# k weights in two blocks of whole rows, and another order of the first four tiles

## The chip, the cores and the metric

The kernel runs on one core of a Trainium2 chip. The metric is device time in microseconds, the median of several executions. The core's engines are TensorE (PE, matmuls and transposes, with its weight loads shown as PEld), VectorE (DVE), ScalarE (ACT), GpSimd (POOL) and SyncE (SP). Each runs its own instructions strictly in the order in which they were written; semaphores make one engine wait for another. Transfers are issued from the queue of an engine, here SP's or ACT's, and are carried out by 16 DMA engines.

## The reference

The input x has 2048 rows of 640 values in bf16. The output is x plus two parts, A and B:

```python
def _A_ref(x, wqkv, wo):            # x: layer norm of the input
    qkv = (x @ wqkv).reshape(B, S, 3, H, Dh)   # 32 heads of 20
    phi = lambda t: jnp.where(t > 0, t + 1, jnp.exp(t)) + 1e-6
    pq, pk = phi(q), phi(k)
    kv = jnp.einsum("bhsd,bhse->bhde", pk, v)
    z = jnp.einsum("bhsd->bhd", pk)
    num = jnp.einsum("bhqd,bhde->bhqe", pq, kv)
    den = jnp.einsum("bhqd,bhd->bhq", pq, z)[..., None] + 1e-6
    return (num / den) @ wo
def _B_ref(x, w_r, w_gate, w_up, w_down):
    r = x @ w_r                     # router; the 8 highest rows
    y = (silu(x_sel @ w_gate) * (x_sel @ w_up)) @ w_down * sigmoid(r_sel)
    return x with y added to the 8 rows chosen
return x + _A_ref(layernorm(x), ...) + _B_ref(x, ...)
```

## The kernel before

The 2048 rows are 16 tiles of 128 rows, t = 0 to 15. In a first phase each tile goes through these steps, each a small Python function:

- `ld` (line 103) loads x of the tile into XX.
- `ln_a`, `ln_b` (151, 154) take the statistics of columns 0 to 319 and 320 to 639 on DVE, `ln_g` (157) joins them, `ln_r` (160, 161) makes the reciprocal deviation with two ACT instructions, `ln_xn` (165) writes the normed tile on DVE.
- `tr_mm` (174) transposes a part of the normed tile on PE into a bank of PSUM (h = 0: two blocks of 128 columns, h = 1: three), and `tr_cp` (181 on ACT, 183 on DVE) copies it to xnT. Tiles 0 to 3 go this way. From tile 4 on `tr_dma` (186) transposes by a DMA on SP's queue.
- `ones` (267) sets one column of the normed tile to one on POOL.
- `K` (210) multiplies xnT of the tile by the k weights wk. It has two halves of 320 output columns (`hs`), in two banks, and each half five matmuls, one per block of 128 weight rows. `KA` is blocks 0 and 1, `KB` blocks 2 to 4. The right half has one more column: the router's weights, put into wk by an ACT copy (line 135) from a transposed w_r.
- `PHe` and `PHr` (226, 229) take exp and relu of a half of K from PSUM on ACT; `PHb` (245) joins both halves to pk on DVE. That is phi(k).
- `G` (254, 261) accumulates the product of the normed tile and pk in PSUM, over all tiles: nine matmuls per tile. `rcopy1` (241) copies tile 1's router column.

For tiles 0 to 3 the order of all these is a list of calls written out by hand, interleaving the tiles; since an engine works in order, the list fixes each engine's order. From tile 4 a loop follows: `K(t)`, `ones(t)`, `PHb(t-1)`, `ln_xn(t+2)` and `tr_dma(t+2)`, `PHe`/`PHr` of t, the statistics of t+3 and t+4, `G(t-1)`. Statistics, norm and transposes of tiles 4 and 5 stand in the list by hand.

After this phase come q (line 482), the key-value products, the experts of part B and the output (line 754). They are not touched. Bank numbers in the list (`6`, `4`, `0`, `2`) say which PSUM bank a step uses, so a bank must be read out before the next matmul starts in it: K of tile 1 uses banks 4 and 5, K of the others 6 and 7, transposes 0 to 3, and G uses banks 0 to 5.

The k weights lie in wk with 768 columns per block of rows. Before the change the left half is in columns 0 to 319, the right one from column 384, and they are loaded as two transfers, the left on ACT's queue, the right on SP's behind x of tiles 1 to 3. Each weight row is a piece of 640 bytes.

Of the kernel before, what the change touches and what calls it, by code (L numbers as in the profile page):

```python
# [7 lines left out]
P = 128  # L8
S = 2048
D = 640  # L10
# [4 lines left out]
KC = D // P  # L15
# [15 lines left out]
F32 = mybir.dt.float32  # L31
I32 = mybir.dt.int32
I16 = mybir.dt.int16
AF = mybir.ActivationFunctionType
# [4 lines left out]
def kernel(  # L39
# [12 lines left out]
    nc = tc.nc  # L52
    pe, dve, act, pool, sp = nc.tensor, nc.vector, nc.scalar, nc.gpsimd, nc.sync

    x_v = A_x[0].rearrange("(t p) d -> p t d", p=P)
    out_v = out[0].rearrange("(t p) d -> p t d", p=P)
    wqkv_v = A_wqkv.rearrange("(kc p) n -> p kc n", p=P)

    sb = ctx.enter_context(tc.tile_pool(name="sb", bufs=1))
    tmp = ctx.enter_context(tc.tile_pool(name="tmp", bufs=2))  # L60
# [6 lines left out]
    def st(shape, dt, name, tag=None):  # L67
        return sb.tile(shape, dt, name=name, tag=tag or name)

    XX = st([P, T, 2, D], BF16, "XX")  # L70
# [3 lines left out]
    wk = st([P, KC, WS], BF16, "wk", "wkM")  # L74
# [21 lines left out]
    MR = st([P, T], F32, "MR")  # L96

    HW = 320
    wkh = [wk[:, :, 0:HW], wk[:, :, HW + 64 :]]


    def ld(eng, dst, src):
        eng.dma_start(dst, src)
# [4 lines left out]
    dve.memset(MVf[:], 0.0)  # L108
    wr = st([KC, P], BF16, "wr")
    ld(act, wr[:], B_w_r.rearrange("(kc p) -> kc p", p=P))  # L110
    ld(act, wkh[0], wqkv_v[:, :, D : D + HW])
    ld(sp, XX[:, 1, 1, :], x_v[:, 1, :])
    ld(sp, XX[:, 2, 1, :], x_v[:, 2, :])
    ld(sp, XX[:, 3, 1, :], x_v[:, 3, :])
    ld(sp, wkh[1][:, :, 0:HW], wqkv_v[:, :, D + HW : 2 * D])
    for a, b in ((4, 8), (8, 12), (12, 16)):
        ld(sp, XX[:, a:b, 1, :], x_v[:, a:b, :])
    sp.dma_start_transpose(xnT[:, 0:4, S - P : S], zero[:])
# [1 line left out]
    def warm4(w):  # L120
# [6 lines left out]
        out=ident[:], in_=ident[:], compare_op=ALU.not_equal, fill=1.0,  # L127
# [18 lines left out]

    sts = {}

    def ln_a(t):
        sts[t] = tmp.tile([P, 2, nc.vector.BN_STATS_DIM], F32, tag="stats", name="stats", bufs=4)  # L150
        dve.bn_stats(out=sts[t][:, 0, :], in_=XX[:, t, 1, 0:320])  # L151

    def ln_b(t):
        dve.bn_stats(out=sts[t][:, 1, :], in_=XX[:, t, 1, 320:D])  # L154

    def ln_g(t):
        dve.bn_aggr(out=MV[:, t, :], in_=sts[t][:])

    def ln_r(t):
        act.activation(lnv[:, t : t + 1], MV[:, t, 1:2], AF.Ln, bias=eps5[:])  # L160
        act.activation(SR[:, t : t + 1], lnv[:, t : t + 1], AF.Exp, scale=-0.5)  # L161

    def ln_xn(t, parts=((0, D),)):
        for a, b in parts:
            dve.tensor_scalar(out=XX[:, t, 0, a:b], in0=XX[:, t, 1, a:b], scalar1=MVf[:, t, 0:1],  # L165
                              scalar2=SR[:, t : t + 1], op0=ALU.subtract, op1=ALU.mult)
# [3 lines left out]
    def tr_mm(t, h, b0):  # L170
        k0, k1 = TRP[h]
        pt = PS[:, b0 + h, :].bitcast(BF16)
        for kc in range(k0, k1):
            pe.transpose(pt[:, (kc - k0) * P : (kc - k0 + 1) * P], XX[:, t, 0, kc * P : (kc + 1) * P], ident[:])  # L174

    def tr_cp(t, h, b0, eng):
        k0, k1 = TRP[h]
        src = PS[:, b0 + h, :].bitcast(BF16)[:, 0 : (k1 - k0) * P].rearrange("p (k c) -> p k c", c=P)
        dst = xnT[:, k0:k1, t * P : (t + 1) * P]
        if eng is act:  # L180
            act.copy(dst, src)
        else:
            dve.tensor_copy(dst, src)

    def tr_dma(t):
        sp.dma_start_transpose(xnT[:, :, t * P : (t + 1) * P], XX[:, t, 0, :])
# [14 lines left out]
    def off(t, h):  # L201
        return T - 1 - t if t != 1 and h else 0

    def K(t, hs=(0, 1), b=6, ks=range(KC)):
        for h in hs:
            if t > 4:
                pad(1)
            w = HW + h
            for kc in ks:
                pe.matmul(  # L210
                    PS[:, b + h, off(t, h) : off(t, h) + w],
                    lhsT=xnT[:, kc, t * P : (t + 1) * P],
                    rhs=wkh[h][:, kc, 0:w],
                    start=(kc == 0),
                    stop=(kc == KC - 1),
                )

    phis = {}

    def phi_src(t, h, b):  # L220
        return PS[:, b + h, off(t, h) : off(t, h) + HW]

    def PHe(t, h, b=6):
        if t not in phis:
            phis[t] = tuple(tmp.tile([P, D], BF16, tag=k, name=k, bufs=3) for k in ("ek", "rk"))
        act.activation(phis[t][0][:, h * HW : (h + 1) * HW], phi_src(t, h, b), AF.Exp)  # L226

    def PHr(t, h, b=6):
        act.activation(phis[t][1][:, h * HW : (h + 1) * HW], phi_src(t, h, b), AF.Relu)  # L229

    def PHa(t, hs=(0, 1), b=6):
        for h in hs:
            PHe(t, h, b)
            PHr(t, h, b)
# [5 lines left out]
    def rcopy1(b):  # L240
        act.copy(rbf[:, T - 2 : T - 1], PS[:, b, HW : HW + 1])

    def PHb(t):
        ek, rk = phis[t]
        dve.scalar_tensor_tensor(out=pk[:, t, :], in0=ek[:], scalar=1.0, in1=rk[:], op0=ALU.min, op1=ALU.add)  # L245

    def pad(n):
        for _ in range(n):
            pe.ldweights(zero[:, 0:P])  # L249

    def G(t, ks=range(KC)):
        for a in ks:
            lhsT = XX[:, t, 0, a * P : (a + 1) * P]
            pe.matmul(  # L254
                PS[:, a, :], lhsT=lhsT, rhs=pk[:, t, 0:512],
                start=(t == 0), stop=(t == T - 1),
            )
            if t > 4:
                pad(2)
            if a < 4:  # L260
                pe.matmul(  # L261
                    PS[:, 5, a * P : (a + 1) * P], lhsT=lhsT, rhs=pk[:, t, 512:D],
                    start=(t == 0 and a == 0), stop=(t == T - 1), skip_group_check=True,
                )

    def ones(t):
        pool.memset(XX[:, t, 0, ZD : ZD + 1], 1.0)  # L267
# [23 lines left out]
    def bm2_copies(gs):  # L291
        for g in gs:
            pool.tensor_copy(bm2[32 * g : 32 * g + 32, :], bm2[0:E2, :])
# [43 lines left out]
    consts_e()  # L337
    bm2_copies((1, 2, 3))
    KA, KB = (range(0, 2), range(2, KC))
    ln_a(0)  # L340
    ln_b(0)
    ln_a(1)
    ln_g(0)
    ln_b(1)
    ln_r(0)
    ln_g(1)
# [5 lines left out]
    tr_cp(0, 0, 0, act)  # L352
    tr_mm(0, 1, 0)
    ones(0)
    ln_a(2)
    tr_mm(1, 0, 2)
    tr_cp(0, 1, 0, act)
    K(0, (0,), 6, KA)
    ln_b(2)
    tr_cp(1, 0, 2, act)  # L360
    tr_mm(1, 1, 2)
    ones(1)
    K(0, (0,), 6, KB)
    tr_cp(1, 1, 2, act)
    ln_g(2)
    ln_a(3)
    K(1, (0,), 4, KA)
    ln_r(2)
    ln_b(3)
    K(1, (0,), 4, KB)  # L370
    PHe(0, 0, 6)
    ln_xn(2)
    K(0, (1,), 6, KA)
    PHr(0, 0, 6)
    K(1, (1,), 4, KA)
    ln_g(3)
    ln_r(3)
    tr_mm(2, 0, 0)
    K(0, (1,), 6, KB)
    tr_cp(2, 0, 0, act)  # L380
    tr_mm(2, 1, 0)
    ones(2)
    ln_xn(3)
    K(1, (1,), 4, KB)
    PHe(0, 1, 6)
    tr_cp(2, 1, 0, dve)
    PHr(0, 1, 6)
    tr_mm(3, 0, 2)
    ln_a(4)
    K(2, (0,), 6, KA)  # L390
    rcopy1(5)
    PHe(1, 0, 4)
    tr_mm(3, 1, 2)
    ones(3)
    PHb(0)
    K(2, (1,), 6, KA)
    PHr(1, 0, 4)
    K(2, (0,), 6, KB)
    PHe(1, 1, 4)
    K(2, (1,), 6, KB)  # L400
    ln_b(4)
    PHr(1, 1, 4)
    PHe(2, 0, 6)
    G(0, (4,))
    tr_cp(3, 0, 2, dve)
    ln_g(4)
    G(0, (0,))
    PHr(2, 0, 6)
    tr_cp(3, 1, 2, dve)
    G(0, (1,))  # L410
    ln_r(4)
    PHb(1)
    G(0, (2,))
    K(3, (0,), 6, KA)
    PHe(2, 1, 6)
    G(0, (3,))
    ln_xn(4)
    PHr(2, 1, 6)
    K(3, (0,), 6, KB)
    ln_a(5)  # L420
    tr_dma(4)
    ones(4)
    K(3, (1,), 6, KA)
    ln_b(5)
    PHe(3, 0, 6)
    G(1)
    PHr(3, 0, 6)
    ln_g(5)
    PHb(2)
    ln_r(5)  # L430
    ln_xn(5)
    K(3, (1,), 6, KB)
    tr_dma(5)
    ones(5)
    G(2)
    PHe(3, 1, 6)
    PHr(3, 1, 6)
    ln_a(6)
    ln_b(6)
    ln_g(6)  # L440
# [515 lines left out]
```

## Time and profile before

| What | Value |
|---|---|
| Median of 3 runs | 106.52 us (106.29 to 106.86) |
| Profiled execution | 106.34 us |
| Its span, first to last instruction | 104.6 us |
| TensorE's granted clock | 1.000 |
| PE busy | 99.7 us, 95% of the span |
| DVE busy | 82.8 us, 79% |
| ACT busy | 68.8 us, 66% |
| Right half of the k weights, issue to landing | 5.4 us |

The profiled execution's time has some 1.7 us around its span. Rows of a timeline give start, duration and what ran, with the idle time before it and what ended that in brackets. The chain of the work that ended last gives at each step the instruction that held up the next one. The profile numbers lines by the kernel's file; a helper has one line for all its calls.

### The profile page before, as it was taken

To read this page: it belongs to the slowest core of one execution; us is meant where nothing else is said; L and a number is where in the kernel's file an instruction comes from. 1 tells how busy PE (TensorE), PEld (TensorE's weight loads), DVE (VectorE), ACT (ScalarE), POOL (GpSimd) and SP (SyncE) were. 2 spreads that over 40 slices of the span, in tenths; PEclk is the share of its full clock that TensorE was granted. 3 is DMA by queue.
4 is the path that set the end of the run, shared out by engine and by line. 5 is a ranking of instruction groups with operands and counts; after the bars stand their busy time and mean duration, and the time that the engine had idled before them with its cause. 6 is when DMAs were issued, how large, how long until landed. Compare 5 with 4: busy or idle time off the path is not lost.

```text
span 104.6 us, 2773 instructions
## 1 busy us (share of the span) xinstructions
PE 99.7 (95%) x916; PEld 72.6 (69%) x1148; DVE 82.8 (79%) x187; ACT 68.8 (66%) x171; POOL 15.9 (15%) x60
## 2 busy tenths in 40 slices
PE   6889999999999999999999999999999999999980
PEld 3257666668888888888777777875567767777760
DVE  1797999988888897873787867878988997888870
ACT  4289957666666666888599999876993996000000
POOL 7800000520000000000000026370000500000140
PEclk9999999999999999999999999999999999999999
DMA  2999938334655555899998999911470136895344
GB/s 67 304 341 382 271 64 58 77 66 96 147 126 101 133 121 117 180 288 337 229 386 282 337 337 379 350 50 39 133 255 9 30 101 205 150 376 211 132 129 125
DMA packets 23024, 19.67 MB, mean 188 GB/s; under 512 B 10594, under 2 KB 21474, under 8 KB 23010
## 3 DMA queue, kind: packets, MB, share of 16 engines
q1 hardware_dynamic: 21880, 19.01, 63.2%
q10 hardware_dynamic: 842, 0.46, 1.6%
q8 instruction: 8, 0.13, 0.5%
q0 software_dynamic: 288, 0.01, 0.3%
q14 instruction: 6, 0.05, 0.1%
HBM read 13.80 MB, written 3.65 MB: 167 GB/s over the span
## 4 chain that ended last, share of the span: by engine, by line
PE 90%; DVE 3%; DMA 2%; issue 1%; DVEq 0%
PE PS L210 21%; PE PS L482 21%; PE PS L754 20%; PE PS L254 15%; PE PS L261 4%; DMA XX<-in_A_x_dram 2%; PE PS L706 2%; PE PS L666 1%; PE PS L548 1%; PE PS L174 1%; PE PS L730 1%; PE PS L677 1%; PE PS L275 1%; DVE stats L151 1%; DVE XX L165 1%
## 5 line engine op out<-in xcount | busy, mean ns | idle before, releaser
L210 PE MATMUL PS<-wk,xnT 128*128 128x320 bf16 (+1 forms) x160 | 25.4, 300 | 0.0
L254 PE MATMUL PS<-pk,XX 128*128 128x512 bf16 x75 | 22.7, 379 | 0.0
L482 PE MATMUL PS<-xnT,wq 128*128 128x512 bf16 x97 | 22.2, 379 | 0.2
L754 PE MATMUL PS<-Mb,pqT 128*128 128x320 bf16 (+4 forms) x165 | 22.1, 295 | 0.0
L249 PEld LDWEIGHTS <-zero 128*128 128x128 bf16 x224 | 18.2, 97 | 5.5
L226 ACT ACTIVATE ek<-PS 128x320 bf16<-128x320 f32 x32 | 14.1, 441 | 9.9 <-PE PS L210 9.9
L754 PEld LDWEIGHTS <-pqT 128*128 128x128 bf16 x165 | 15.8, 98 | 4.7 <-issue 0.3
L210 PEld LDWEIGHTS <-xnT 128*128 128x128 bf16 x160 | 15.2, 97 | 4.7 <-issue 0.2
L245 DVE SCALAR_TENSOR_TENSOR pk<-ek,rk 128x640 bf16<-128x640 bf16 x16 | 13.1, 819 | 4.8 <-ACT rk L229 4.5
L539 DVE SCALAR_TENSOR_TENSOR pqT<-qe,qr 128x512 bf16<-128x512 bf16 x20 | 13.5, 685 | 2.9 <-ACT qr L491 2.9
L490 ACT ACTIVATE qe<-PS 128x512 bf16<-128x512 f32 x20 | 12.3, 616 | 3.2 <-PE PS L482 3.2
L261 PE MATMUL PS<-pk,XX 128*128 128x128 bf16 x64 | 14.0, 219 | 0.3
L229 ACT ACTIVATE rk<-PS 128x320 bf16<-128x320 f32 x32 | 14.0, 438 | 0.0
L482 PEld LDWEIGHTS <-wq 128*128 128x128 bf16 x100 | 11.6, 118 | 2.9 <-issue 0.2
L491 ACT ACTIVATE qr<-PS 128x512 bf16<-128x512 f32 x20 | 12.3, 616 | 0.0
L763 DVE TENSOR_TENSOR o<-PS,XX 128x640 bf16<-128x640 f32 x11 | 9.0, 822 | 2.9 <-PE PS L754 2.0
L254 PEld LDWEIGHTS <-XX 128*128 128x128 bf16 x80 | 7.8, 98 | 4.5
L198 ACT ACTIVATE XX<-XX,MR,SR 128x640 bf16<-128x640 bf16 x11 | 9.4, 913 | 0.0
L151 DVE BATCH_NORM_STATS2 stats<-XX 128x6 f32<-128x320 bf16 x16 | 7.4, 461 | 1.9 <-DMA XX<-in_A_x_dram 1.9
L165 DVE TENSOR_SCALAR XX<-XX,MVf,SR 128x640 bf16<-128x640 bf16 (+2 forms) x17 | 7.2, 432 | 0.6 <-ACT SR L161 0.6
L154 DVE BATCH_NORM_STATS2 stats<-XX 128x6 f32<-128x320 bf16 x16 | 7.7, 480 | 0.0
L267 POOL MEMSET XX<- 128x1 bf16 x18 | 1.8, 102 | 35.7 <-DVE XX L165 20.2
(114 smaller groups left out, 100.0 us busy)
## 6 DMA issues: line engine op xcount, KB each, us to landing
out_dram<-o SPq DMA_DIRECT2D x15, 160.0 KB, 2.0
XX<-in_A_x_dram SPq DMA_DIRECT2D x3, 640.0 KB, 7.9
wg<-in_B_w_gate_dram SPq DMA_DIRECT2D x5, 384.0 KB, 8.6
wu<-in_B_w_up_dram SPq DMA_DIRECT2D x5, 384.0 KB, 6.1
wd<-in_B_w_down_dram SPq DMA_DIRECT2D x1, 1920.0 KB, 10.6
wv<-in_A_wqkv_dram SPq DMA_DIRECT2D x5, 160.0 KB, 3.1
wq<-in_A_wqkv_dram SPq DMA_DIRECT2D x1, 800.0 KB, 5.9
hi_d<-XX SPq DMA_DIRECT2D x1, 800.0 KB, 4.0
```

The source lines that it names most:

```text
L210: pe.matmul(PS[:, b + h, off(t, h) : off(t, h) + w], lhsT=xnT[:, kc, t * P : (t + 1) * P], rhs=wkh[h][:, kc, 0:w], start=(kc == 0), stop=( ...
L226: act.activation(phis[t][0][:, h * HW : (h + 1) * HW], phi_src(t, h, b), AF.Exp)
L229: act.activation(phis[t][1][:, h * HW : (h + 1) * HW], phi_src(t, h, b), AF.Relu)
L245: dve.scalar_tensor_tensor(out=pk[:, t, :], in0=ek[:], scalar=1.0, in1=rk[:], op0=ALU.min, op1=ALU.add)
L249: pe.ldweights(zero[:, 0:P])
L254: pe.matmul(PS[:, a, :], lhsT=lhsT, rhs=pk[:, t, 0:512], start=(t == 0), stop=(t == T - 1),)
L261: pe.matmul(PS[:, 5, a * P : (a + 1) * P], lhsT=lhsT, rhs=pk[:, t, 512:D], start=(t == 0 and a == 0), stop=(t == T - 1), skip_group_check= ...
L482: pe.matmul(PS[:, bank, :], lhsT=by5(wq[:, kc, :])[:, m, :], rhs=xnT[:, kc, tb * TBLK : (tb + 1) * TBLK], start=(kc == 0), stop=(kc == KC ...
L490: act.activation(e, PS[:, bank, :], AF.Exp)
L491: act.activation(r, PS[:, bank, :], AF.Relu)
L539: dve.scalar_tensor_tensor(out=pqT[:, m, tb * TBLK : (tb + 1) * TBLK], in0=e, scalar=1.0, in1=r, op0=ALU.min, op1=ALU.add,)
L754: pe.matmul(PS[:, b, o : o + c1 - c0], lhsT=pqT[:, kc, t * P : (t + 1) * P], rhs=Mb[:, kc, c0:c1], start=(kc == 0), stop=(kc == KC - 1))
```

## The change

The weights lie in wk as whole rows of 640 columns, with the router's column behind them. They are loaded as two transfers on ACT's queue: block rows 0 and 1, then 2 to 4; each piece is 1280 bytes. SP's queue carries x of tiles 1 to 3 and then the larger transfers of x. The list of calls for tiles 0 to 3 is in another order; its calls are the same ones. Two small helpers (`st_of`, `er`) let either half of the statistics, and either of exp and relu, come first.

```diff
-    wkh = [wk[:, :, 0:HW], wk[:, :, HW + 64 :]]
+    wkh = [wk[:, :, 0:HW], wk[:, :, HW:]]
...
-    ld(act, wkh[0], wqkv_v[:, :, D : D + HW])
-    ld(sp, XX[:, 1, 1, :], x_v[:, 1, :])
-    ld(sp, XX[:, 2, 1, :], x_v[:, 2, :])
-    ld(sp, XX[:, 3, 1, :], x_v[:, 3, :])
-    ld(sp, wkh[1][:, :, 0:HW], wqkv_v[:, :, D + HW : 2 * D])
+    for a, b in ((0, 2), (2, KC)):
+        ld(act, wk[:, a:b, 0:D], wqkv_v[:, a:b, D : 2 * D])
+    for t in (1, 2, 3):
+        ld(sp, XX[:, t, 1, :], x_v[:, t, :])
...
+    ln_b(0)
     ln_a(0)
-    ln_b(0)
...
     ones(0)
-    ln_a(2)
+    ln_b(2)
     tr_mm(1, 0, 2)
     tr_cp(0, 1, 0, act)
     K(0, (0,), 6, KA)
-    ln_b(2)
+    ln_a(2)
     tr_cp(1, 0, 2, act)
     tr_mm(1, 1, 2)
     ones(1)
-    K(0, (0,), 6, KB)
+    K(0, (1,), 6, KA)
     tr_cp(1, 1, 2, act)
     ln_g(2)
+    K(0, (0,), 6, KB)
     ln_a(3)
+    ln_r(2)
+    K(1, (1,), 4, KA)
+    ln_b(3)
     K(1, (0,), 4, KA)
...
```

From there the new list, without its `ones` calls, reads by engine:

```
PE:  K(0) right KB, K(1) left KB, tr_mm(2,0), K(1) right KB, tr_mm(2,1),
     tr_mm(3,0), K(2) left KA, tr_mm(3,1), K(2) right KA, left KB, right KB,
     G(0) blocks 0, 2, 1, 4, K(3) left KA, G(0) block 3, K(3) right KA,
     left KB, right KB, G(1), G(2), then the loop with K(4)
ACT: PHe(0,0), PHr(0,0), ln_r(3), PHr(0,1), tr_cp(2,0), PHe(0,1), rcopy1,
     PHe(1,1), PHr(1,0), PHr(1,1), PHe(1,0), PHe(2,0), PHr(2,0), PHr(2,1),
     PHe(2,1), ln_r(4), PHr(3,0), PHe(3,0), PHe(3,1), PHr(3,1), ln_r(5)
DVE: ln_g(3), ln_xn(2), ln_xn(3), tr_cp(2,1), tr_cp(3,0), PHb(0), ln_b(4),
     ln_a(4), tr_cp(3,1), ln_g(4), PHb(1), ln_xn(4), ln_a(5), ln_b(5),
     PHb(2), ln_g(5), ln_xn(5), ln_a(6), ln_b(6), ln_g(6), then the loop
SP:  tr_dma(4) behind ln_xn(4), tr_dma(5) behind ln_xn(5)
```

The old list has on PE K(0) left before K(0) right, K(1) left before the right halves, G(1) between the halves of K(3), and G(0) in the order 4, 0, 1, 2, 3; on ACT ln_r(4) ahead of PHe(2,1) and PHr(2,1), and ln_r(5) ahead of PHe(3,1); on DVE ln_a(4), PHb(0) and ln_b(4) between the copies of tile 2 and tile 3, and ln_g(5) ahead of PHb(2).

More of the change, by code (lines that the diff above doesn't have):

```diff
@@ L147, with st_of @@
     sts = {}
+    def st_of(t):
+        if t not in sts:
+            sts[t] = tmp.tile([P, 2, nc.vector.BN_STATS_DIM], F32, tag="stats", name="stats", bufs=4)
+        return sts[t]
     def ln_a(t):
-        sts[t] = tmp.tile([P, 2, nc.vector.BN_STATS_DIM], F32, tag="stats", name="stats", bufs=4)
-        dve.bn_stats(out=sts[t][:, 0, :], in_=XX[:, t, 1, 0:320])
+        dve.bn_stats(out=st_of(t)[:, 0, :], in_=XX[:, t, 1, 0:320])
     def ln_b(t):
-        dve.bn_stats(out=sts[t][:, 1, :], in_=XX[:, t, 1, 320:D])
+        dve.bn_stats(out=st_of(t)[:, 1, :], in_=XX[:, t, 1, 320:D])
     def ln_g(t):
@@ L221, in phi_src, with er, PHe @@
         return PS[:, b + h, off(t, h) : off(t, h) + HW]
-    def PHe(t, h, b=6):
+    def er(t):
         if t not in phis:
             phis[t] = tuple(tmp.tile([P, D], BF16, tag=k, name=k, bufs=3) for k in ("ek", "rk"))
-        act.activation(phis[t][0][:, h * HW : (h + 1) * HW], phi_src(t, h, b), AF.Exp)
+        return phis[t]
+    def PHe(t, h, b=6):
+        act.activation(er(t)[0][:, h * HW : (h + 1) * HW], phi_src(t, h, b), AF.Exp)
     def PHr(t, h, b=6):
-        act.activation(phis[t][1][:, h * HW : (h + 1) * HW], phi_src(t, h, b), AF.Relu)
+        act.activation(er(t)[1][:, h * HW : (h + 1) * HW], phi_src(t, h, b), AF.Relu)
     def PHa(t, hs=(0, 1), b=6):
@@ L362 @@
     ones(1)
-    K(0, (0,), 6, KB)
+    K(0, (1,), 6, KA)
     tr_cp(1, 1, 2, act)
     ln_g(2)
+    K(0, (0,), 6, KB)
     ln_a(3)
+    ln_r(2)
+    K(1, (1,), 4, KA)
+    ln_b(3)
     K(1, (0,), 4, KA)
-    ln_r(2)
-    ln_b(3)
-    K(1, (0,), 4, KB)
[L371 to L376, printed above, removed]
+    PHe(0, 0, 6)
+    K(0, (1,), 6, KB)
+    ln_g(3)
+    PHr(0, 0, 6)
+    ln_xn(2)
+    K(1, (0,), 4, KB)
     ln_r(3)
     tr_mm(2, 0, 0)
-    K(0, (1,), 6, KB)
+    PHr(0, 1, 6)
+    K(1, (1,), 4, KB)
+    ln_xn(3)
     tr_cp(2, 0, 0, act)
@@ L382 @@
     ones(2)
-    ln_xn(3)
-    K(1, (1,), 4, KB)
     PHe(0, 1, 6)
+    tr_mm(3, 0, 2)
+    K(2, (0,), 6, KA)
     tr_cp(2, 1, 0, dve)
[L387 to L390, printed above, removed]
     rcopy1(5)
-    PHe(1, 0, 4)
+    PHe(1, 1, 4)
     tr_mm(3, 1, 2)
     ones(3)
-    PHb(0)
+    tr_cp(3, 0, 2, dve)
     K(2, (1,), 6, KA)
     PHr(1, 0, 4)
+    PHb(0)
     K(2, (0,), 6, KB)
-    PHe(1, 1, 4)
+    PHr(1, 1, 4)
     K(2, (1,), 6, KB)
+    PHe(1, 0, 4)
     ln_b(4)
-    PHr(1, 1, 4)
     PHe(2, 0, 6)
+    G(0, (0,))
+    ln_a(4)
+    G(0, (2,))
+    PHr(2, 0, 6)
+    G(0, (1,))
+    tr_cp(3, 1, 2, dve)
+    PHr(2, 1, 6)
     G(0, (4,))
-    tr_cp(3, 0, 2, dve)
     ln_g(4)
[L407 to L410, printed above, removed]
+    PHe(2, 1, 6)
+    PHb(1)
+    K(3, (0,), 6, KA)
     ln_r(4)
[L412 to L415, printed above, removed]
     G(0, (3,))
+    K(3, (1,), 6, KA)
     ln_xn(4)
-    PHr(2, 1, 6)
     K(3, (0,), 6, KB)
     ln_a(5)
+    K(3, (1,), 6, KB)
     tr_dma(4)
     ones(4)
-    K(3, (1,), 6, KA)
+    PHr(3, 0, 6)
     ln_b(5)
+    G(1)
     PHe(3, 0, 6)
-    G(1)
-    PHr(3, 0, 6)
+    PHb(2)
+    PHe(3, 1, 6)
+    PHr(3, 1, 6)
     ln_g(5)
-    PHb(2)
     ln_r(5)
+    G(2)
     ln_xn(5)
-    K(3, (1,), 6, KB)
     tr_dma(5)
     ones(5)
-    G(2)
-    PHe(3, 1, 6)
-    PHr(3, 1, 6)
     ln_a(6)
```

## The prediction

> **What bounds the kernel now.** I read the page first (its chain that ended last), then that chain in order of time over the first 20 us, then the timelines of ScalarE (ACT), VectorE (DVE) and SyncE (SP) in that stretch, and last the DMA queues in short windows. The page:
>
> ```profile
> span 104.6 us, 2773 instructions
> PE 90%; DVE 3%; DMA 2%; issue 1%; DVEq 0%
> ```
>
> TensorE (PE) is 90% of the chain (last line). The change touches only the start, so what counts is how much time PE loses there. The chain, start and length in us:
>
> ```profile
> 3.64 0.39 DVE stats L154
> ...
> 6.24 0.29 PE PS L174 x2
> 6.53 0.27 PE PS L210 x2
> 6.80 0.17 PE PS L174 x3
> 6.97 1.15 PE PS L210 x8
> 8.12 0.03 issue
> 8.15 0.71 PE PS L210 x4
> ...
> 16.86 1.36 PE PS L210 x10
> 18.23 0.22 PE PS L254
> ...
> 19.53 0.54 PE PS L210 x4
> ```
>
> L174 is a transpose, L210 a matmul of K, L254 and L261 those of G. From 6.24 PE is in the chain without a break. One K matmul is 1.36/10 = 0.136 us, one G is 19.53 - 18.23 = 1.30, one transpose 0.17/3 = 0.057. From 6.53 to K(4) at 16.86 PE has 40 K matmuls (5.44), 13 transposes (0.74) and G(0) to G(2) (3.90), together 10.08, in 10.33 us. So at most 0.25 us can be packed away there; before 6.24 the chain is the load and the layer norm of tiles 0 and 1, where the change only swaps two equal DVE instructions, and x of tiles 0 and 1 stays first on SP. A gain over 0.5% (0.53 us) has no place to come from; a loss has.
>
> **The loads.** Issues and landings, and queue rows (packets, MB, share of 16 engines; q10 is ACT's queue, q1 SP's) in the windows 3.5 to 4, 4.375 to 4.5, 5.625 to 5.75 and 7.5 to 8:
>
> ```profile
> 1.45 0.41 ACTq L103 DMA_DIRECT2D wk<-in_A_wqkv_dram  x1
> wk<-in_A_wqkv_dram ACTq DMA_DIRECT2D x1, 400.0 KB, 4.6
> 1.74 0.90 SPq L103 DMA_DIRECT2D XX<-in_A_x_dram  x2
> 2.68 0.43 SPq L103 DMA_DIRECT2D wk<-in_A_wqkv_dram  x1
> wk<-in_A_wqkv_dram SPq DMA_DIRECT2D x1, 400.0 KB, 5.4
> 3.89 0.18 ACT L135 COPY wk<-PS 128x5 bf16<-128x5 bf16 x1 [1.81 <-PE PS L133]
> ...
> q10 hardware_dynamic: 203, 0.13, 93.7%
> q1 hardware_dynamic: 2, 0.00, 1.4%
> ...
> q1 hardware_dynamic: 18, 0.02, 51.9%
> q10 hardware_dynamic: 29, 0.02, 45.2%
> ...
> q10 hardware_dynamic: 1, 0.00, 0.5%
> ...
> q1 hardware_dynamic: 145, 0.18, 108.0%
> ```
>
> Before, the right half lands at 2.68 + 5.4 = 8.1, just where the chain has its 0.03 of issue and starts the right half of tile 0 at 8.15. *ACT's second issue* costs 0.41 us of ACT at 1.9 to 2.3; the 1.81 us idle ahead of the copy L135 hides it, and without that cover it would be 0.41 on ACT. *SP's issue that goes* (0.43) lets x of tiles 4 to 7 start that much earlier. The copy L135 also writes a column of wk: before, it ran at 3.89 while the other weights of wk were still landing, so it doesn't wait for them; zero.
>
> *Longer rows.* A 640-byte row takes 0.5 x 0.937 x 16 / 203 = 37 ns of an engine, a 1280-byte row (x) 0.5 x 16 / 145 = 55 ns. Weights are 1280 rows of the first kind before and 640 of the second after: 2.96 us of all engines become 2.2.
>
> *When block B (rows 2 to 4) lands.* ACT's queue begins its weights at about 2.9, 1.45 after the issue. It needs 40 rows of 55 ns per engine. Upper case: alone for 0.5 us, then sharing half and half with SP's queue (as 4.375 to 4.5 shows, 45 to 52% of the time): 2.9 + 0.5 + 2 x 1.7 = 6.8, and 0.35 from last packet to landing (5.7 against 1.45 + 4.6), and up to 0.45 for the slowest engine: 7.15 to 7.6. Lower case: SP's x waits behind the weights issued earlier (at 3.5 to 4 SP's queue moved 2 packets though x of tile 2 was issued at 1.74): 48 rows, 2.9 + 2.64 + 0.35 = 5.9. I take 7.4, near the upper end, because that row shows both queues full.
>
> The Trainium skill, "DMA: Bandwidth & Descriptors", Queues, rings and completion order, says an engine drains a whole packet of some 9 to 17 descriptors of one ring before it turns to the next. By that, block B would land at an estimated 6.3 (56 rows ahead of its end) and never be late; no row here shows how long one turn is.
>
> When is B wanted? New PE order: transposes of tile 0, two of tile 1 (6.24), K(0) left KA at 6.53, three transposes, K(0) right KA at 6.97, K(0) left KB at 6.97 + 2 x 0.136 = 7.24. Landing at 7.4 holds PE for 0.16. Block A is wanted at 6.53 and is done long before: its 16 rows per engine with the 8 of x of tile 2 beside them take 24 x 0.055 = 1.3, so 2.9 + 1.3 + 0.35 + 0.45 = 5.0.
>
> **The new order, step by step.** PE, without waits, from 7.24: K(0) left KB to 7.65, four of K(1) to 8.19, K(0) right KB to 8.60, K(1) left to 9.01, two transposes, K(1) right to 9.53, then eight transposes (0.46) and K(2) (1.36) to 11.35; G(0) starts. ACT and DVE rows that price it:
>
> ```profile
> 7.82 0.42 ACT L226 ACTIVATE ek<-PS 128x320 bf16<-128x320 f32 x1
> 8.13 0.43 ACT L229 ACTIVATE rk<-PS 128x320 bf16<-128x320 f32 x1
> 8.54 0.29 ACT L160 ACTIVATE lnv<-MVf,eps 128x1 f32<-128x1 bf16 x1
> 9.00 0.37 ACT L181 COPY xnT<-PS 128x256 bf16<-128x256 bf16 x1
> 9.41 0.44 ACT L226 ACTIVATE ek<-PS 128x320 bf16<-128x320 f32 x1
> 12.01 0.37 ACT L160 ACTIVATE lnv<-MVf,eps 128x1 f32<-128x1 bf16 x1
> ...
> 9.58 0.36 DVE L183 COPY xnT<-PS 128x384 bf16<-128x384 bf16 x1
> 11.99 0.81 DVE L245 SCALAR_TENSOR_TENSOR pk<-ek,rk 128x640 bf16<-128x640 bf16 x1
> 12.72 0.44 DVE L165 TENSOR_SCALAR XX<-XX,MVf,SR 128x640 bf16<-128x640 bf16 x1
> ```
>
> ACT's starts are 0.32 apart for an exp or relu (8.13 less 7.82), 0.46 for ln_r (9.00 less 8.54), 0.41 for a transposed copy. Walked from PHr(0,0) at 8.13: ln_r(3) 8.45, PHr(0,1) 8.91, copy 9.23, PHe(0,1) 9.64, rcopy1 9.96, then eight of 0.32 (PHe(1,1) to PHe(2,1)) from 10.00 to 12.56, ln_r(4) from 12.56 to 13.09. DVE, with 0.39 for a bn_stats, 0.73 for a PHb (12.72 less 11.99) and 0.36 for a copy: xn(3) 9.02, copies 9.74 and 10.07, PHb(0) 10.3 to 11.1, bn of tile 4 to 11.8, copy, PHb(1) 12.16 to 12.9. So PHb(0) is done before PE wants it (11.1 against 11.35) and each bank is read out before it is reused; PE runs on: G(0) and K(3) mixed to 14.02, G(1) to 15.32, G(2) to 16.62, K(4) there instead of at 16.86. That is the 0.24 that could be packed away.
>
> What is late next? ln_r(4) stands behind PHr(2,1) and PHe(2,1): 12.56 instead of 12.01, so xn(4) starts at 13.13 instead of 12.72, bn of tile 5 and PHb(2) follow to 15.05, and bn_aggr(5) now stands behind PHb(2). ln_r(5) is then at 15.3, xn(5) at 15.87, bn of tile 6 to 17.2, PHb(3) 17.27 to 18.1. G(3) wants PHb(3) at 16.62 + 1.36 = 17.98: it waits to about 18.14, against 18.23 before. **Sum: -0.09 us.** The 0.16 for block B fits under this same wait (PE has 0.16 to spare before G(3)), and ACT would shift by 0.04.
>
> **SP's queue: transposes.** Tiles 4 and 5 go through DMA transposes right behind xn.
>
> ```profile
> 13.19 1.20 SPq L186 DMA_TRANSPOSE xnT<-XX  x1
> 15.90 0.10 POOL L267 MEMSET XX<- 128x1 bf16 x1 [5.24 <-DMA xnT<-XX]
> 15.30 1.21 SPq L186 DMA_TRANSPOSE xnT<-XX  x1
> xnT<-XX SPq DMA_TRANSPOSE x1, 3.9
> 19.19 0.68 PEld L210 LDWEIGHTS <-xnT 128*128 128x128 bf16 x5
> ```
>
> Tile 4: issued 13.60, and 15.90 - 13.19 = 2.7 later 16.3: 0.3 ahead of K(4). Tile 5: issued 16.33, at 2.7 there at 19.03; K(5) loads its weights at 18.14 + 1.30 - 0.2 = 19.25. Before, tile 5 took 3.9 and still came in time (15.30 + 3.9 = 19.2). Covered by 0.2 at 2.7, not covered at 3.9.
>
> The right half of wk now starts at column 320 instead of 384. The output matmuls read their tile at the same 320 already: 299 ns each, as K's.
>
> ```profile
> L754 PE MATMUL PS<-Mb,pqT 128*128 128x320 bf16 x109 | 15.0, 299 | 0.0
> L210 PE MATMUL PS<-wk,xnT x160: 297/299/310, 6.4 to 47.2; 128*128 128x320 bf16 x80, 128*128 128x321 bf16 x80
> ```
>
> So zero. After G(3) everything is as before, DVE catching up within two tiles.
>
> **Rivals.** *Transposes of tile 5 late (slower).* If they take 3.9 again, they land at 16.33 + 3.9 = 20.23 and K(5) stands 1.0 us: 106.34 - 0.09 + 1.0 = 107.25 in the profiled execution, about 107.4 as median. It passes 0.5% from 3.5 us on. For it: the one row at 3.9. Against: tile 4's 2.7. *Block B late.* At 7.6 to 8.0 PE stands 0.4 to 0.8, of which 0.16 is absorbed: 106.5 to 106.9, median 106.7 to 107.1; still within 0.5% but for the end. For it: shared queues; against: the empty q1 at 3.5 to 4. *Packed fully.* PHb(3) isn't late and no wait arises: -0.25, median 106.3. *The loads aren't the matter:* B is in time, and the old order's wait at 8.12 was only 0.03, so the load part alone moves nothing; this agrees with the forecast in time.
>
> **How the numbers follow.** The profiled execution took 106.34, 0.18 under the median 106.52. My sum gives 106.25 there and 106.4 as median. About 0.5% (0.53 us) is what a measurement here can tell from no change. Chances: the forecast (106.2 to 106.6) 0.48, block B late 0.22, tile 5's transposes late 0.18, packed fully 0.12. From these: faster by over 0.5% only where something ahead of 6.24 also shrinks, 0.06; slower, tile 5 and the worst of block B, 0.21; same 0.73. The range reaches from full packing and the spread of the runs, 105.9, to tile 5 with about 0.8 of wait, 107.2.
>
> **What would show it.** Right: both weight blocks landed by about 7.4; K(4) in the chain at 16.6 to 16.7; ln_r(4) near 12.6; xn(5) near 15.9; a DVE wait of 0.1 to 0.2 ahead of G(3). Wrong: an issue or DMA wait of PE at 7.24 over 0.3 us; a gap ahead of K(5) near 19.3; or a new ACT wait between 7.8 and 13, where its row leaves no slack.

## The result, and the profile after

The changed kernel took 106.99 us as median of 20 runs (106.39 to 108.01), the kernel before, measured beside it, 106.38 (20 runs, 106.23 to 106.9). The ratio is 1.0044, with a 95% interval of 1.0028 to 1.0061: slower by 0.3 to 0.6%, where the prediction had 0.1 us faster. In a few executions of several kernels below the granted clock fell or the time stood far above the others; the ratios leave those out, so they need not be the quotient of the medians.

The profiled execution of the changed kernel took 107.52 us, 0.53 above its median, so its wait is probably one of the longer ones. The chain in order of time over the first stretch (start and length in us; L213 is now a matmul of K, L177 a transpose, L260 one of G):

```profile
1.87 0.03 issue
1.90 6.46 DMA wk<-in_A_wqkv_dram
8.36 0.04 issue
8.40 1.93 PE PS L213 x13
...
17.93 1.36 PE PS L213 x10
19.29 0.32 PE PS L260
...
20.70 1.36 PE PS L213 x10
```

The chain runs over the load of the second weight block, from its issue to 8.36, before PE goes on. K(4) starts at 17.93 instead of 16.86. The page, PE's timeline and the landing times show the same place:

```profile
PE 88%; DMA 6%; issue 1%; DVE 1%; ACT 1%; ACTq 0%; DVEq 0%
L213 PE MATMUL PS<-wk,xnT 128*128 128x320 bf16 (+1 forms) x160 | 25.0, 299 | 1.0 <-DMA wk<-in_A_wqkv_dram 1.0
```

```profile
6.96 0.44 PE L213 MATMUL PS<-wk,xnT 128*128 128x321 bf16 x2
8.40 1.93 PE L213 MATMUL PS<-wk,xnT 128*128 128x320 bf16 x13 [1.00 <-DMA wk<-in_A_wqkv_dram]
```

```profile
wk<-in_A_wqkv_dram ACTq DMA_DIRECT2D x1, 480.0 KB, 6.5
wk<-in_A_wqkv_dram ACTq DMA_DIRECT2D x1, 320.0 KB, 4.0
```

K(0) right KA, the last work ahead of block B in the new order, begins at 6.96; K(0) left KB begins at 8.40, after 1.0 us in which PE waits for block B. B was issued at 1.90 and took 6.46.

In the same execution x of tile 2 was late too. DVE, which starts its statistics at 6.10 in the kernel before, waited for it:

```profile
7.02 0.49 DVE L157 BATCH_NORM_STATS2 stats<-XX 128x6 f32<-128x320 bf16 x1 [0.68 <-DMA XX<-in_A_x_dram]
```

### The profile page after: what moved, and what is told of

It is laid out like the page before. It is cut to its first block, busy times and chain, and to the rows that moved or that the text cites. A ratio compares the mean times of both kernels' runs of the same rounds, so it can differ in the third digit from the quotient of the medians.

```text
span 105.8 us, 2780 instructions
## 1 busy us (share of the span) xinstructions
PE 100.8 (95%) x924; PEld 72.9 (69%) x1148; DVE 82.6 (78%) x187; ACT 69.1 (65%) x171; POOL 16.4 (16%) x60
## 4 chain that ended last, share of the span: by engine, by line
PE 88%; DMA 6%; issue 1%; DVE 1%; ACT 1%; ACTq 0%; DVEq 0%
PE PS L488 21%; PE PS L213 20%; PE PS L760 19%; PE PS L260 16%; DMA wk<-in_A_wqkv_dram 6%; PE PS L267 3%; PE PS L712 2%; PE PS L672 1%; PE PS L554 1%; PE PS L736 1%; PE PS L683 1%; PE PS L281 1%; DVE o L773 1%; PE PS L634 1%; ACT L106 1%
## 5 line engine op out<-in xcount | busy, mean ns | idle before, releaser
L213 PE MATMUL PS<-wk,xnT 128*128 128x320 bf16 (+1 forms) x160 | 25.0, 299 | 1.0 <-DMA wk<-in_A_wqkv_dram 1.0
L260 PE MATMUL PS<-pk,XX 128*128 128x512 bf16 x80 | 23.4, 379 | 0.0
L213 PEld LDWEIGHTS <-xnT 128*128 128x128 bf16 x160 | 15.3, 98 | 5.5 <-issue 1.2
L260 PEld LDWEIGHTS <-XX 128*128 128x128 bf16 x80 | 7.8, 98 | 4.5
```

The source lines that it names most:

```text
L213: pe.matmul(PS[:, b + h, off(t, h) : off(t, h) + w], lhsT=xnT[:, kc, t * P : (t + 1) * P], rhs=wkh[h][:, kc, 0:w], start=(kc == 0), stop=( ...
L260: pe.matmul(PS[:, a, :], lhsT=lhsT, rhs=pk[:, t, 0:512], start=(t == 0), stop=(t == T - 1),)
```

## The experiments

I began with two theories: L, that block B lands late because x of tiles 2 to 7 on SP's queue shares the engines with it, the large transfers for tiles 4 to 7 above all; and O, that the new order itself costs the time, through ln_r(4) and xn(5).

**The loads alone.** The new loads and the new place in wk, and the old list of calls.

> The new loads and the new place of the weights in wk, with the old order of tiles 0 to 3. Theory L (block B lands at about 8.36 us because it shares the DMA engines with x of tiles 2 to 7, and PE stands for it): the old order wants block B at 6.97 already, for the last three matmuls of K(0) left, so PE stands about 1.4 us there, and since nothing is in front of the second half that would not fit, the kernel is 0.8 to 1.4 us slower than before (107.2 to 107.8). Theory O (the new order itself costs the time, through ln_r(4) and xn(5) being late): with the old order the loads alone are harmless, within 0.2 us of before.

Median 107.82, ratio 1.0075 (1.0042 to 1.0107). Theory O alone is out: with the old order the loads cost something as well, 0.8 us by the ratio, the low end of what L gave. In the profile PE stood 1.63 us ahead of K(0) left KB, and block B landed 0.04 before it went on. The profile names ACT's ln_r(2) for that wait, which ended at the same moment because x of tile 2 was late here too, but these matmuls don't read it. In three of 13 executions TensorE's granted clock fell, and the profiled one is of these; the rows are in the last section.

**The order alone.** The old loads, the new list.

```diff
-    for a, b in ((0, 2), (2, KC)):
-        ld(act, wk[:, a:b, 0:D], wqkv_v[:, a:b, D : 2 * D])
+    ld(act, wkh[0], wqkv_v[:, :, D : D + HW])
...
+    ld(sp, wkh[1][:, :, 0:HW], wqkv_v[:, :, D + HW : 2 * D])
```

> The old loads (left half on ACT's queue, right half on SP's behind x of tiles 1 to 3, 640-byte rows) with the new order. Theory L: the new order wants the right half at 6.97 instead of 8.15, and it lands at about 8.1, so PE stands some 1.1 us: 0.6 to 1.1 us slower than before (107.0 to 107.5), about as slow as the whole change. Theory O: slower as well, by the same amount as the whole change (0.6 us), but with the wait ahead of G(3) or K(5) and not ahead of K(0) right. The place of the wait tells them apart.

Median 107.5, ratio 1.0083 (1.0052 to 1.0115). PE's waits in its profile:

```profile
7.00 0.43 PE L214 MATMUL PS<-wk,xnT 128*128 128x320 bf16 x2 [0.50 <-DMA wk<-in_A_wqkv_dram]
8.62 3.88 PE L214 MATMUL PS<-wk,xnT 128*128 128x321 bf16 x15 [1.02 <-DMA wk<-in_A_wqkv_dram]
```

The longer wait stands ahead of K(0) right, as L said and O did not. A wait of 0.50 ahead of K(0) left comes before it, which neither theory named: the left half landed at 6.96 in this execution, against 6.0 in the kernel before. This profile, too, is of an execution in which the clock fell, so its 15 matmuls take 3.88 us. By the middle of their ratios each half of the change is worse alone than both together, but the intervals overlap with that of the whole (1.0028 to 1.0061). What is clear is that neither half is free.

**The large transfers of x behind the weights, on ACT's queue**, with the new and with the old order.

```diff
-        ld(sp, XX[:, a:b, 1, :], x_v[:, a:b, :])
+        ld(act, XX[:, a:b, 1, :], x_v[:, a:b, :])
```

> The whole change, and the three large transfers of x (tiles 4 to 15) issued on ACT's queue behind the two weight blocks instead of on SP's queue, so that they cannot share the engines with the weights. Theory L: block B lands by about 7.2, the wait of 1.0 us ahead of K(0) left KB is gone or under 0.2, and the time is 106.2 to 106.4, 0.5 to 0.8 us under the changed kernel. Theory O, or a theory that ACT's queue or the 1280-byte rows are slow in themselves: block B still lands after 8, or the wait goes and the time stays near 107.

> The same loads as in the run with the large transfers of x behind the weights, but with the old order of tiles 0 to 3. Theory L: block B is wanted at 6.97 and lands by about 7.2, so PE stands 0.1 to 0.3 us: 106.4 to 106.7, a little slower than the new order with the same loads by 0.1 to 0.3. Theory O: the old order is the better one with the same loads, by 0.5 us or more.

110.31 (ratio 1.0182, 1.0101 to 1.0262, from two of six executions) and 109.13 (1.0226, 1.0182 to 1.0269, from four of six): the times don't tell the theories apart, because the edit made a new wait. ACT's timeline of the first:

```profile
3.13 4.05 ACTq L103 DMA_DIRECT2D XX<-in_A_x_dram  x3
7.23 0.18 ACT L134 COPY wk<-PS 128x5 bf16<-128x5 bf16 x1 [5.14 <-DMA XX<-in_A_x_dram]
```

The last of these issues had to wait until x of tile 2 had landed (to 6.8), since both count on the same semaphore in this program, and ACT's own work, the router's column and ln_r(0), is queued behind it. The landing of block B can be read all the same: 8.4 (1.89 + 6.5) and 8.0 (1.89 + 6.1), where L said 7.2. Moving the large transfers behind the weights did not bring block B forward.

**The large transfers of x held on SP's queue.** GpSimd writes one column of the target of x of tile 4; the transfers are issued behind that write, the first at 5.37.

```diff
-    for a, b in ((4, 8), (8, 12), (12, 16)):
-        ld(sp, XX[:, a:b, 1, :], x_v[:, a:b, :])
...
     bm2_copies((1, 2, 3))
+    pool.memset(XX[:, 4, 1, 0:1], 0.0)
+    for a, b in ((4, 8), (8, 12), (12, 16)):
+        ld(sp, XX[:, a:b, 1, :], x_v[:, a:b, :])
```

> The whole change, with the three large transfers of x (tiles 4 to 15) left on SP's queue but held until about 5.2 us, by a one-column write of GpSimd into their target ahead of them; ACT's queue stays as it is in the change. Theory L (block B is late because its tail shares the engines with x of tiles 4 to 7): block B lands by about 7.3 instead of 8.36, PE waits under 0.2 us ahead of K(0) left KB, 106.3 to 106.5. Rival W (the weights and x of tiles 1 to 3 alone are too much for the engines by then, or the tail is in ACT's queue itself): block B lands at 8 or later and the time stays at 106.9 to 107.1.

The profile did what L said: block B landed at 1.88 + 5.5 = 7.4, PE waited for nothing there, and that execution took 106.51. Part of that is luck: x of tile 1 landed later here, so PE began K(0) at 6.67 instead of 6.52 and wanted block B at 7.38 instead of 7.24. The median did not follow: 106.91, ratio 1.0015 (0.9982 to 1.0048), which can't be told from before, and hardly from the changed kernel.

**Block B wanted later.**

```diff
-    K(0, (0,), 6, KB)
     ln_a(3)
     ln_r(2)
     K(1, (1,), 4, KA)
     ln_b(3)
     K(1, (0,), 4, KA)
+    K(0, (0,), 6, KB)
```

> The whole change, with one move in the order: the four matmuls of K(1) KA (0.54 us) ahead of K(0) left KB, so that block B is wanted at 7.78 instead of 7.24. If the wait for block B sets the loss, PE's wait shrinks from 1.0 to about 0.5 and the time by 0.3 to 0.5 us, to 106.5 to 106.7. If ln_r(4), xn(5) and the DVE chain set it, nothing changes: 106.9 to 107.1, since exp of K(0) left comes no earlier.

PE's wait shrank to 0.6, but the median was 107.24, ratio 1.0038 (1.001 to 1.0067), which can't be told from the changed kernel: the second of the two outcomes. The chain tells why:

```profile
1.88 6.49 DMA wk<-in_A_wqkv_dram
8.37 0.04 issue
8.41 0.58 PE PS L213 x3
9.00 0.02 issue
9.02 0.44 ACT ek L232
9.46 0.33 ACT rk L235
9.78 0.19 ACT lnv L163
9.97 0.02 issue
10.00 0.21 ACT SR L164
10.21 0.03 issue
10.23 0.46 DVE XX L168
```

From block B the chain goes through the exp of K(0) left, ACT's queue (ln_r(3) is behind it) and xn(3). Giving PE other work doesn't help when the result that B completes is what ACT stands for.

**Block B not loaded**, with the new and the old order.

```diff
-    for a, b in ((0, 2), (2, KC)):
-        ld(act, wk[:, a:b, 0:D], wqkv_v[:, a:b, D : 2 * D])
+    ld(act, wk[:, 0:2, 0:D], wqkv_v[:, 0:2, D : 2 * D])
+    dve.memset(wk[:, 2:KC, 0:D], 0.0)
```

> The whole change, but block B of the k weights (rows 2 to 4 of five) is not loaded; VectorE writes zeros there at the start, in its idle time. The output leaves that part of K out. This shows the new order with no wait for weights. Theory L: PE never waits for block B, K(4) starts at 16.6 to 16.7 in the chain, and the time is 106.2 to 106.4: the order itself is worth 0 to 0.1. Theory O (the order is slower by itself): 106.6 or more, with a wait ahead of G(3) or K(5).

> The same with the old order: block A loaded as in the change, block B not loaded but zeroed at the start, the order of tiles 0 to 3 as before; that part of K is left out of the output. Theory L: within 0.1 us of before (106.3 to 106.5), since the old order had only 0.25 us of slack between 6.53 and K(4), and at most 0.2 slower than the new order with block B zeroed. Theory O: faster than the new order with block B zeroed by 0.3 or more.

106.51 (ratio 0.9988, 0.9967 to 1.0008) with the new order, 106.59 (0.9992, 0.9966 to 1.0019) with the old one. Without that load neither order can be told from before, nor from the other.

**PE kept busy in its wait**, in the kernel with the loads alone.

```diff
     ones(1)
+    for _ in range(3):
+        warm4(512)
     K(0, (0,), 6, KB)
```

> The new loads with the old order, as in the first run, and three idle matmuls of 512 columns on PE (the same as those at the start of the kernel) ahead of K(0) left KB, so that PE works through its wait. In that first run PE idled 1.63 us, the granted clock then was 0.68 from 8 to 10 and 0.50 from 10 to 12, and a K matmul took 0.27 us instead of 0.136. Theory C (the idle time itself brings the clock down): the clock stays at 1.0 in those stretches, and the time falls from 107.8 to about 107.2. Theory D (the clock falls for another reason, such as the load of the DMA engines): the clock still falls and the time stays at 107.8 or above.

The clock stayed at 0.998 or above in all six executions, as C said. The time did not fall as C said: 109.84 (1.0309, 1.0273 to 1.0345). The idle matmuls took 2.64 us, a microsecond more than the wait, and in the profile the transposes of tile 4 then took 4.66 us and K(4) waited 1.0 for them. What the fallen clock alone costs is not measured by this. With three low clocks in 13 executions, six without one come about by chance one time in five, so this run alone does not show that the idling was the cause.

**The kernel before with the large transfers held.** The same edit in the old kernel.

> The kernel before, with the three large transfers of x held until about 5.2 us in the same way as in the earlier run. Theory L: its right half, which lands at 8.1 and is wanted at 8.12, lands somewhat earlier; only the 0.03 to 0.1 of wait there can go, so the time is 0 to 0.1 us under before, and its longer times (up to 107.6) become rarer. If the large transfers of x were wanted earlier than they then land, it would be slower, with a DVE wait ahead of bn_stats of tile 4 near 11.

106.85, ratio 1.0019 (0.9992 to 1.0045): nothing gained, and its times still reach 107.4.

**Block B in two halves**, the left one first, as the change has it and with the large transfers held.

```diff
-    for a, b in ((0, 2), (2, KC)):
-        ld(act, wk[:, a:b, 0:D], wqkv_v[:, a:b, D : 2 * D])
+    ld(act, wk[:, 0:2, 0:D], wqkv_v[:, 0:2, D : 2 * D])
+    for c in (0, HW):
+        ld(act, wk[:, 2:KC, c : c + HW], wqkv_v[:, 2:KC, D + c : D + c + HW])
```

> The whole change, with block B loaded as two transfers on ACT's queue, its left half (wanted at 7.24) ahead of its right half (wanted at 8.19), rows of 640 bytes in both. Theory L: the left half lands about 0.7 to 1.0 us ahead of 8.36, so the wait ahead of K(0) left KB falls from 1.0 to 0.1 to 0.5, and the time is 106.5 to 106.8. If the shorter rows cost more than the split gains, the right half lands after 9 and PE waits ahead of K(0) right KB instead: 107 or more.

> Both together: block B in two halves, left first, and the large transfers of x held until about 5.2 us. Theory L: nothing waits for weights any more; as the order alone is worth nothing that could be measured, the time is that of before within 0.2 us, 106.3 to 106.6, and 0.1 to 0.4 under the run that only held x. If it stays at 106.9, the held x is itself the cause of what that run lost.

109.36 (1.029, 1.0232 to 1.0348) and 106.86 (1.0015, 0.9987 to 1.0043). In the first, the fourth issue on ACT's queue only came at 3.19, when x of tile 0 had landed (it counts on the same semaphore), and the right half landed at 9.67, 6.48 later; PE then waited 1.48 for it. In the second nothing waited for weights in the profile, yet the median is no better than with the large transfers held alone. By its expectation the held x would then be a cost of its own. The kernel before with the same hold has a ratio of the same size, 1.0019, and neither is clear of no change, so that stays open.

**The changed kernel, the large transfers held, and block B not loaded, side by side on one chip.** The time with the large transfers held did not fit its profile, so these three were run again together.

> The changed kernel once more, beside the two runs that take away its wait, on one chip. Its ratio to before should be 1.003 to 1.007 again, with a wait of PE for block B ahead of K(0) left KB of 0.5 to 1.2 us.

> The changed kernel with the large transfers of x held until about 5.2 us, once more. Theory L (block B's tail shares the engines with x of tiles 4 to 7): at least half of the changed kernel's loss is gone, a ratio to before of 0.999 to 1.002, and no wait for block B in the profile. Rival W (the early loads as a whole are too much): the same ratio as the changed kernel within 0.1%.

> The changed kernel with block B zeroed instead of loaded (its output leaves that part of K out), once more. Theory L: a ratio of 0.997 to 1.001. Theory O (the order itself costs time): 1.003 or more.

1.0051 (1.0016 to 1.0086), 1.0057 (1.0031 to 1.0082) and 1.0011 (0.9991 to 1.0032). The changed kernel's profile has a wait of 0.4, just under the expected 0.5 to 1.2. Holding back the large transfers gains nothing here, 0.06% from the changed kernel as rival W said: theory L falls as it was stated, and the 106.51 of the first profile was one good execution. What is not excluded is that x of tiles 4 to 7 shares the engines with block B's last rows, for the hold ends at 5.37 and block B landed after 8. Not loading block B does take the loss away. In the profile with the large transfers held block B now landed at 8.53, and PE waited 1.3 for it. Its chain, and the rows of ACT's queue (q10: packets, MB, share of 16 engines) in the windows 6.5 to 7, 7 to 7.5, 7.5 to 8 and 8 to 8.5:

```profile
1.88 6.65 DMA wk<-in_A_wqkv_dram
8.53 0.04 issue
8.57 1.93 PE PS L210 x13
```

```profile
q10 hardware_dynamic: 52, 0.06, 32.9%
...
q10 hardware_dynamic: 12, 0.01, 7.1%
...
q10 hardware_dynamic: 8, 0.01, 5.5%
...
q10 hardware_dynamic: 4, 0.00, 2.2%
```

One engine is 1/16, 6.25%. From 7.0 on the share and the 24 rows left over 1.2 us are those of about one engine working off the rest.

**x of tiles 2 and 3 held too, and block B ahead of them on SP's queue.** The rivals now: W, the early loads as a whole are too much by the time at which they are wanted; T, an engine or two trail whatever is beside the weights.

```diff
-    for t in (1, 2, 3):
+    for t in (1,):
         ld(sp, XX[:, t, 1, :], x_v[:, t, :])
...
+    pool.memset(XX[:, 2, 1, 0:1], 0.0)
+    for t in (2, 3):
+        ld(sp, XX[:, t, 1, :], x_v[:, t, :])
```

```diff
-    for a, b in ((0, 2), (2, KC)):
-        ld(act, wk[:, a:b, 0:D], wqkv_v[:, a:b, D : 2 * D])
-    for t in (1, 2, 3):
+    ld(act, wk[:, 0:2, 0:D], wqkv_v[:, 0:2, D : 2 * D])
+    ld(sp, XX[:, 1, 1, :], x_v[:, 1, :])
+    ld(sp, wk[:, 2:KC, 0:D], wqkv_v[:, 2:KC, D : 2 * D])
+    for t in (2, 3):
         ld(sp, XX[:, t, 1, :], x_v[:, t, :])
```

> The whole change, with x of tiles 2 and 3 held until about 5.2 us as well, ahead of the large transfers of x, so that from 3 to 6 us the two weight blocks have the DMA engines nearly alone. This kernel must be slow, since statistics of tile 2 then start near 7.5 or later; what counts is when block B lands. Theory W (the early loads as a whole are too much for the engines): block B lands by 6.0 to 6.6. Theory T (one or two of the sixteen engines trail behind the others, whatever is beside the weights): the last rows of ACT's queue still trickle for 1 us or more, and block B lands at 7 or later.

> The whole change, with block B on SP's queue behind x of tile 1 and ahead of x of tiles 2 and 3, block A on ACT's as it is. Theory W: block B lands by 7.0 or so, since x of tiles 2 and 3 comes behind it; x of tile 2 then lands at 7 or later, DVE waits for it, and the time is 106.7 to 107.2. Theory T: block B lands no earlier than 7.4 here either.

107.75 (1.0126, 1.008 to 1.0172) and 107.62 (1.0125, 1.0055 to 1.0194). Of the first, the DMA issue of block B, DVE's timeline and PE's:

```profile
wk<-in_A_wqkv_dram ACTq DMA_DIRECT2D x1, 480.0 KB, 5.0
```

```profile
7.62 0.49 DVE L154 BATCH_NORM_STATS2 stats<-XX 128x6 f32<-128x320 bf16 x1 [1.48 <-DMA XX<-in_A_x_dram]
```

```profile
6.75 2.21 PE L210 MATMUL PS<-wk,xnT 128*128 128x321 bf16 x15
```

Of the second, PE's and DVE's timelines:

```profile
6.72 2.21 PE L214 MATMUL PS<-wk,xnT 128*128 128x321 bf16 x15
10.05 0.29 PE L178 MATMUL PS<-ident,XX 128*128 128x128 bf16 x2 [1.13 <-DVE XX L169]
```

```profile
7.36 0.49 DVE L158 BATCH_NORM_STATS2 stats<-XX 128x6 f32<-128x320 bf16 x1 [1.26 <-DMA XX<-in_A_x_dram]
```

In both, PE runs from K(0) right KA to K(1) left KB, 15 matmuls on end, with no wait for block B. It landed at 1.88 + 5.0 = 6.9 in the first and, by the trace, at 6.96 in the second. Now x of tile 2 is late instead (DVE starts its statistics at 7.4 to 7.6), and PE stands 1.1 us for tile 2's transposes. The second run agrees with W's landing (7.0) against T's (7.4), though its time is above W's 106.7 to 107.2. The first fits neither: 6.9 is later than W's 6.0 to 6.6 and just short of T's 7. Its rows of ACT's queue in the windows 5.5 to 6 and 6 to 6.5:

```profile
q10 hardware_dynamic: 61, 0.07, 36.2%
...
q10 hardware_dynamic: 30, 0.03, 18.3%
```

From 5 to 5.5 the queue still had 154 rows, and SP's queue moved nothing from 4 to 6. So the weights had the engines to themselves, and still the last rows took a microsecond on some six, then three of 16 engines. Both theories are part of the cause: with less beside it block B comes earlier, as W said, and some engines trail even with nothing beside it, as T said. In these two runs and in the changed kernel PE waits for whatever of block B and x of tile 2 is late.

## Why the prediction was wrong

**The step that failed** is the landing of block B: "7.15 to 7.6", "I take 7.4". In five profiles with these loads and this order of transfers it landed at 8.36 and 7.74 (the changed kernel), 8.37 (block B wanted later), and 7.4 and 8.53 (the large transfers held). The mechanism was right, a wait of PE ahead of K(0) left KB; the mis-sized term of the sum is the "0.45 for the slowest engine", for which the prediction names no row. The trace holds 16 updates of a transfer's semaphore, as many as there are engines, and the last of them is the landing. For block B, and for the right half of the kernel before, in us:

| Profile | Middle of the 16 | 15th | Last |
|---|---|---|---|
| Changed kernel | 6.67 | 7.58 | 8.36 |
| Changed kernel, side by side | 6.64 | 7.42 | 7.74 |
| Large transfers held | 6.62 | 7.29 | 7.37 |
| Large transfers held, side by side | 6.80 | 7.55 | 8.53 |
| x of tiles 2 and 3 held too | 5.96 | 6.77 | 6.84 |
| Block B on SP's queue | 6.02 | 6.35 | 6.96 |
| Kernel before, right half | 7.11 | 7.62 | 8.10 |

My sum had the typical engine at 7.15 and the slowest 0.45 later. With the changed kernel's loads, held or not, the middle came earlier, at 6.6 to 6.8, and the last 0.8 to 1.7 after it. The last rows of ACT's queue in the changed kernel start 0.05 apart up to 8.0, each 0.055 long: one engine, one row after the other. The kernel before already had such a tail, 1.0 for its right half (above) and 1.0 for its left half (4.96 to 6.00). Block A was late by the same term, 5.45 against my 5.0, without cost because it was wanted at 6.53. That one landing came near my 7.4 is luck: two errors of opposite sign.

**A second step failed, the price of the wait:** it "fits under this same wait" ahead of G(3). The last run without block B has the same order and no wait. Against it the changed kernel starts K(0) left KB 1.17 later (8.40 against 7.23), K(4) 1.33 later and K(5) 1.30 later. Only 0.03 was swallowed, since the wait also shifts ACT and DVE: PHb(3) started at 18.41 instead of 17.12, and G(3) waited for it again. And 0.16 came on top. After a wait 13 K matmuls took 1.93 us, while 15 in a stream took 2.04; the first one takes 0.299, the others 0.136 each. One small slip changes nothing: 8.13 less 7.82 is 0.31, not 0.32.

Behind the landing lies a sum that I did not make: x of tiles 0 to 3 (655 KB) and both weight blocks (819 KB) are all wanted by 7.24 in the new order. In the kernel before only x and the left half, 1065 KB, are wanted by then, and the other 410 KB at 8.15. At the prediction's 145 rows per half microsecond, 1474 KB are 1152 rows of 1280 bytes, or 4.0 us. They start at about 2, which makes 6.0, and 0.35 more to landing. By this estimate 0.9 is left before 7.24, and the last engine's tail alone is of that size; what x of tiles 4 to 7 takes comes on top.

**The rival "Block B late"** is what happened: 7.6 to 8.0, median 106.7 to 107.1, measured 106.99. I gave it 0.22. Its price was 0.3 too low, by the second step: it gives 106.59 for a landing at 7.74 and 107.21 for one at 8.36, and these two profiled executions took 106.92 and 107.52. In the second of them PE would not have run on even with block B in time: tile 2's norm ended at 9.45, and without a wait PE wants it at 9.0.

**The rule of the Trainium skill** on turns of 9 to 17 descriptors, by which an estimated 6.3 came out and B was never late ("DMA: Bandwidth & Descriptors", Queues, rings and completion order): block B landed at 8.36. Half of its updates had come by 6.67, nearer to that estimate than to my 7.15, but the last ones decide. No row shows the length of a turn, so whether the rule holds here stays open.

**The order** came out as walked. In the last run without block B the first K matmul is at 6.52, K(4) at 16.60 and K(5) at 19.40:

```profile
6.52 0.27 PE PS L213 x2
...
16.60 1.36 PE PS L213 x10
19.40 1.36 PE PS L213 x10
```

From first to K(4) that is 10.08 (10.33 before; 10.08 was the packed sum), and from K(4) to K(5) 2.80 where 2.67 is steady: the wait ahead of G(3), 0.13 against 0.16 forecast. To K(5) it is 12.88 against 13.00 before, so 0.12 less where I had 0.09. Too little to measure: 1.0011 and 0.9988.

**What else was right or not reached.** ACT's second issue cost nothing (its copy still ran at 3.89, with 1.80 idle ahead). Column 320 cost nothing (299 ns per K matmul, as before). The transposes of tile 5, the rival on which I put my slower case, landed 2.8 after the issue; they did not come late. *Packed fully* was stopped by G(3), as the sum said. *The loads aren't the matter* was wrong: without block B no loss is left that could be measured.

The forecast of no change (within 0.5%) covers the ratio's middle; the sign was wrong.

## What to carry to other kernels

Before an order is changed at the start of a kernel, list for each early transfer when the new order wants it, and add up the bytes that are wanted by then: the old order's gap between its first and its second weights was what let 410 KB arrive late. A landing is set by the last of the sixteen engines, not by the typical one; here it came 0.8 to 1.7 us after it and varied by a microsecond from one execution to the next, so a single profile without a wait proves little. A slack further on swallows a wait only if the work that makes the slack does not wait as well. Loads and order should be tried apart and with the disputed transfer left out; here each half alone cost time too, which a run of the whole would not have told.

## What the runs showed of the hardware that I had not expected

**TensorE's clock was halved for 3.4 us after PE had stood for 1.6 us.** In the profiled execution of the loads alone, PE idled from 7.0 to 8.65. Windows of that profile (busy times of PE, PEld, DVE, ACT, POOL, then granted clock, DMA share and GB/s):

```profile
6.00:8.00 2.00, 0.95 (x10) 0.59 (x9) 1.07 (x3) 1.50 (x4) 0.20 (x2) 1.00 1.06 383
8.00:10.00 2.00, 1.35 (x6) 0.80 (x6) 1.48 (x6) 0.90 (x4) 0.00 (x0) 0.68 1.07 376
10.00:12.00 2.00, 2.00 (x11) 1.17 (x10) 0.45 (x1) 0.74 (x4) 0.00 (x0) 0.50 1.08 356
```

```profile
8.65 3.31 PE PS L213 x12
```

Twelve K matmuls took 3.31 us, 0.276 each instead of 0.136. By the trace the granted clock was 0.50 from 8.73 to 12.14 and 1.00 around that. PE had been busy 1.71 of the 3.41 us before. In the profile of the order alone the clock was 0.50 from 8.70 to 12.11, and PE had been busy 1.81 of the 3.41 us before. In the first run with block B in halves it was busy 1.92 of 3.40 us around its wait, and the clock stayed at 1.00.

Three of the 13 executions of the loads alone had a mean clock of 0.983 or 0.984 and took 109.49 to 109.81, the others 106.77 to 107.97. Such clocks were commoner where PE stands longer in the profile: 7 of 12 executions with the large transfers on ACT's queue (waits over 2 us), 2 of 6 with block B in halves alone (1.5), and none of 28 of the changed kernel (1.0 and 0.4). But 2 of 105 executions of the kernel before and 1 of 24 with the new order and no block B had one too, and their profiles show no such wait. So that idling brings the clock down is likely, but not shown, and it may not be the only cause. With PE kept busy through the same wait the clock stayed at 0.998 or above in all six.

The Trainium skill, "TensorE: Matmul & The Clock Gate", Part 1, states half rate after an idle window of about 3.4 us. The two halved stretches above have that length, but a window in which PE stood for half was enough; the measurement decides.

**A DMA transpose is not always 2.7 us.** It took 2.6 to 2.8 in most rows, but 3.9 for tile 5 before and 4.66 for tile 4 with the idle matmuls. What lengthens it is left open.

**Which engine trails, and why, is left open**: the trace counts 16 updates and rows per queue, but names no engine, and no run took a single engine out.
